# Eight attention pairs scored on row halves, weight splits on VectorE, and another slot order in the expert stage

## The chip, the cores and the metric

One NeuronCore of a Trainium2 chip runs the whole program. The metric is the device time of one execution in microseconds (us); lower is better. A profiled execution gives a trace beside its time. A change of 0.5%, about 4 us here, is what a measurement of this kernel can tell from none.

## The reference

Three stages, each fed by the one before it.

```
# attention: q, k, v are (4, 12, 448, 64)
scores = cap * tanh(q @ k.T / sqrt(64) / cap)
attn = exp(scores - max) / (sum + 1e-9);  x = attn @ v
# dense layer: x (1792, 768), w_in (768, 1024), w_out (1024, 768)
h = x @ w_in;  s = h * softmax(h);  ln = (s - mean) / sqrt(var + 1e-6) * g_ln
x = ln @ w_out
# experts: 8 of them, one per token
e = argmax(x @ w_gate + modality_bias[modality_id])
out = probs[e] * (relu(x @ w1[e]) @ w2[e])
```

w_in and w_out arrive as 64-bit floats.

## The kernel before, in words

**Attention** walks over 24 pairs of heads (batch b, pair p, n = 6b + p). `a_load` fetches K and Q of a pair, head dimension on the partitions; two heads of 64 fill 128. `a_sc` makes scores for one head j and two of four key chunks of 112 keys (cp selects the two), ScalarE (ACT) turns them by Tanh and Exp into a tile "e" (L688, L689), and `a_av` multiplies e by V (L710, tile "av") and sums the exponentials into the tile "S": directly with a 0/1 matrix ("zone") where `direct` holds (n < 6, L718), or, for later pairs, over sums that VectorE (DVE) and GpSimd (POOL) formed first (L695 to L699, L726).

Products on TensorE (PE) are either plain fp32 or split into a rounded fp32r part and a remainder. `a_split` makes these for K (tiles kh, kl) and Q (qs, high part above and low part below). Pairs 0 and 1 are "plain": fp32, K stored twice on the two partition halves, Q with zeros in the lower half. Pair 2 is in `HALF`: both heads in one tile, split, three products on 64 partitions each. Pairs 3 to 23 are split, two products of 128 partitions per chunk.

**Weights.** While the first pairs run, 12 pieces of w_in and 16 of w_out are loaded by POOL's queue and turned to fp32 by three DVE instructions (`f64_to_f32`, L433 to L435). `conv_in` then rounds (L459, ACT, two on DVE) and forms the remainder winl on POOL (L460). `conv_out` does it with g_ln folded in (L478 or L480, then L481), `conv_tr` transposes the piece on PE (L490, tile "pt") and copies it out (L492), `conv_og` forms eight gate columns (L498, tile "po"; L499, L500). `CUS` says behind which half pair each piece stands. The tables KHA, QSA, KLP, QLP, ESP, CIN, COUT, WTD name the engine of each piece of work.

**Dense layer.** Once a batch's six pairs are done (`a_fin1`, `a_fin2`), its token tiles are cut into small steps, which `fill` puts between the attention products of later pairs: h = x w_in (L540 to L542), activation, transposes, y = ln w_out (L590 to L592). Up to here a scheduler sets each engine's order from the program; from the expert stage on the program's order is kept.

**Experts.** A busiest expert's first tokens go first; then the slots of `STATIC` follow: D (4 x 128 tokens), F (2 x 128), H (128), each with its own expert's w1 and w2 loaded by the SP queue, rounded on ACT (L1025) and the remainder on DVE (L1026). `SMALL` hangs two slots T of 32 tokens on slots 0 and 2. A slot is: transposes of the gathered tokens (`s_tr`, tiles xtD, xtH, xtF, L1056), the first product (`s_h`, L1079 to L1081, tile phD or phF; for H `s_hh`, L1099 to L1101, followed by transposes `s_ht`, tile htH, L1115), the second product (`s_o`, L1146 to L1148, tiles poD, poH, poF). A T slot has `t_tr` (tile tpT, L1170), `t_h` (thT, L1181), `t_ht` (ttT, L1191, copied to hTT, L1193) and `t_o` (toT, L1204). `run_slots` sets their order; the transposes of the next slot stand between the two products of the present one.

Every engine takes its instructions in order; the ring of tiles "e" has 4 buffers, scores and most other PSUM tiles share 3.

Of the kernel before, what the change touches and what calls it, by code (L numbers as in the profile page):

```python
# [10 lines left out]
F32 = mybir.dt.float32  # L11
# [53 lines left out]
HALF = (2,)  # L65
BIN = 0
BOUT = -1
QLP = (1, 8, 10, 11, 13)
CIN = (1, 5)
# [3 lines left out]
FFIRST = 0  # L73
KHA = (6, 7, 8, 11)
QSA = (2, 8, 11, 15, 23)
KLP = (4, 5, 6, 8, 9, 10, 12, 13, 15, 16, 18, 19, 22, 23)
ESP = (3, 5, 6, 7, 9, 19, 20, 21, 22)
XHA = (0, 2, 3, 5, 7, 9, 11, 12)
XLP = (1, 3, 4, 6, 9, 10)
WTD = (1, 2, 6, 8, 12, 14, 15)  # L80
XCD = (6, 7, 9, 10, 12, 13, 14, 15, 16, 17, 18, 19, 20)
QACT = 0
VACT = 0
COUT = (0, 2, 3, 4, 5, 6, 8, 9, 10, 11, 12, 14)
CUS = (0, 3, 3, 3, 4, 4, 5, 5, 5, 5, 5, 6, 7, 7, 8, 8, 9, 9, 10, 11, 11, 12, 12, 13, 13, 14, 14, 15, 16, 17)
# [5 lines left out]
def attn_moe_kernel(ctx, tc, qt, kt, vv, cap, w_in, w_out, g_ln, ids, w_gate, mbias, w1, w2, out):  # L91
# [357 lines left out]
    def conv_in(k, hf):  # L449
        raw = mp.tile([P, 512, 2], I32, tag="m4", name=f"rawi{k}_{hf}", bufs=4)  # L450
        pool.dma_start(out=raw, in_=w_in[k * P:(k + 1) * P, hf * 512:(hf + 1) * 512]
                     .bitcast(I32).rearrange("p (f t) -> p f t", t=2))
        t = mp.tile([P, 512], I32, tag="x3", name=f"ti{k}_{hf}", bufs=4)
        f64_to_f32(t, raw)
        tf = t.bitcast(F32)
        h_, l_ = winh[k][:, hf * 512:(hf + 1) * 512], winl[k][:, hf * 512:(hf + 1) * 512]

        def rest():
            (dve.tensor_copy if (2 * k + hf) in CIN else act.copy)(h_, tf)  # L459
            pool.tensor_sub(l_, tf, h_)  # L460

        defer(BIN, rest)
# [3 lines left out]
    def conv_out(c, hf):  # L466
# [8 lines left out]

        def rest():
# [4 lines left out]
            dve.scalar_tensor_tensor(l_, tf, g_t[:, c:c + 1], h_, op0=ALU.mult, op1=ALU.subtract)  # L481

        defer(BOUT, rest)
        wT[c, hf] = tf

    def conv_tr(c, hf):
# [5 lines left out]
        (dve.tensor_copy if 2 * c + hf in WTD else act.copy)(tt, pt[:, :3 * P].rearrange("p (a b) -> p a b", a=3))  # L492
# [119 lines left out]
    def plain(b, p):  # L612
        return b * NP + p < PLAIN and b * NP + p not in HALF

    def a_load(b, p):
        k, q = [], []
        if b * NP + p in HALF:
            for l, src, nm in ((k, kt, "k"), (q, qt, "q")):
                t = ap_.tile([P, S], F32, tag="raw", name=f"{nm}r{b}_{p}", bufs=4)
                sp.dma_start(out=t, in_=src[b, p].rearrange("j d s -> (j d) s"))  # L620
                l += [t, t]
            raws[b, p] = (k, q)
            return
# [18 lines left out]
    def a_split(b, p, js=(0, 1)):  # L642
        k, q = raws[b, p]
        spl.setdefault((b, p), [])
        for j in js:
            n = b * NP + p
            if n in HALF:
                if j == js[0] and not spl[b, p]:
                    kh = ap_.tile([P, S], F32R, tag="kh", name=f"kh{b}_{p}", bufs=3)
                    kl = ap_.tile([P, S], F32R, tag="kl", name=f"kl{b}_{p}", bufs=3)  # L650
                    qh = ap_.tile([P, S], F32R, tag="qs", name=f"qh{b}_{p}", bufs=3)
                    ql = ap_.tile([P, S], F32R, tag="qs", name=f"ql{b}_{p}", bufs=3)
                    (act.copy if n in KHA else dve.tensor_copy)(kh, k[j])
                    (act.copy if n in QSA else dve.tensor_copy)(qh, q[j])
                    (pool if n in KLP else dve).tensor_sub(kl, k[j], kh)
                    (pool if n in QLP else dve).tensor_sub(ql, q[j], qh)
                    spl[b, p] = [(kh, kl, (qh, ql))] * 2
                continue
            if plain(b, p):
                spl[b, p].append((k[j], None, q[j]))  # L660
                continue
# [3 lines left out]
            n = b * NP + p  # L665
# [7 lines left out]

    def a_sc(b, p, j, cp):
        kh, kl, qs = spl[b, p][j]
        ps = atile(f"sc{b}_{p}_{j}_{cp}")
        for c in range(2):
            k0 = (2 * cp + c) * CK
            if b * NP + p in HALF:
                r = slice(64 * j, 64 * j + 64)  # L680
                for i, (x, y) in enumerate(((kh, qs[0]), (kl, qs[0]), (kh, qs[1]))):
                    pe.matmul(ps[:CK, c, :S], x[r, k0:k0 + CK], y[r], start=(i == 0), stop=(i == 2))
                continue
            pe.matmul(ps[:CK, c, :S], kh[:, k0:k0 + CK], qs, start=True, stop=plain(b, p))  # L684
            if not plain(b, p):
                pe.matmul(ps[:CK, c, :S], kl[:, k0:k0 + CK], qs, start=False, stop=True)  # L686
# [14 lines left out]
    avt, spt = {}, {}  # L701

    def a_av(b, p, cp):
        if cp == 0:
            avt[b, p] = btile(f"av{b}_{p}")
        o = avt[b, p]
        v = vt[b, p]
        for c in range(2):
            for j in range(2):
                pe.matmul(o[64 * j:64 * j + 64, :S], v[:, 2 * cp + c, 64 * j:64 * j + 64],  # L710
                          et[b, p, j, cp][:, c, :], start=(cp == 0 and c == 0), stop=(cp == 1 and c == 1))
        if cp == 0 and p == 0:
            spt[b] = psS.tile([P, 512], F32, tag="S", name=f"S{b}")
        if direct(b, p):
            for j in range(2):
                for c in range(2):
                    g = 2 * j + c
                    pe.matmul(spt[b][32 * g:32 * g + 32, :S], zone[:, 31 - p:63 - p], et[b, p, j, cp][:, c, :],  # L718
                              start=(p == 0 and cp == 0), stop=(p == NP - 1 and cp == 1))
        if cp == 1:  # L720
            (dve.tensor_copy if b * NP + p in XCD else act.copy)(xtile(b)[:, p, :], o[:, :S])
        if cp == 1 and p % 2 and not direct(b, p):
# [669 lines left out]
```

## Time and profile before

| | |
|---|---|
| median of 3 runs | 815.36 us (812.24 to 815.41) |
| profiled execution, its own time | 816.4 us |
| its span, first to last instruction | 814.6 us |
| PE busy | 770.6 us (95%) |
| DVE busy | 478.4 us (59%) |
| ACT busy | 389.8 us (48%) |
| POOL busy | 260.1 us (32%) |
| mean granted PE clock | 0.97 of full |

Shares of the whole span are averages over stages with different limits. The view by windows gives each engine's busy time in a stretch, and the granted clock of PE there; a mean clock between 0.5 and 1 is a mixture of its two levels, 1.2 and 2.4 GHz. The durations of matmuls in the trace overlap, since they are pipelined: what one costs in a row of them is the distance between starts.

### The profile page before, as it was taken

The numbers are of one execution on the slowest core, as the hardware profiler recorded it, in microseconds if no ns is written. First come the engines' busy times: TensorE is split into PE (matmuls) and PEld (weight loads), VectorE is DVE, ScalarE is ACT, GpSimd is POOL, SyncE is SP. The second block draws the span as 40 slices with busy tenths as digits, with TensorE's granted clock in tenths as the row PEclk, the third lists the DMA queues.
The fourth block names the chain that finished last, engine by engine and source line by source line (L and its number), as shares of the span: only waits on it lengthen the run. The fifth ranks groups of instructions, "written<-read, shape, count | busy, mean of one in ns | idle before, by whom it ended". The sixth has DMA issues, their size and how long they took to land.

```text
span 814.6 us, 11543 instructions
## 1 busy us (share of the span) xinstructions
PE 770.6 (95%) x4158; PEld 593.0 (73%) x4158; DVE 478.4 (59%) x843; ACT 389.8 (48%) x539; POOL 260.1 (32%) x325
## 2 busy tenths in 40 slices
PE   7888989999999999999999999899999989999983
PEld 2324545676677877577769799799879978799982
DVE  4999897757764566675435755756146171461730
ACT  5665853766755545656651224434144252442530
POOL 3763244544443342438623213441200101001000
PEclk9979979999999999999999999999999989999997
DMA  7866532123322222223000302467928259382711
GB/s 187 253 190 188 175 110 55 47 76 99 97 70 65 77 57 76 88 63 94 12 20 20 138 20 97 153 229 245 387 81 258 104 201 394 130 259 103 239 66 42
DMA packets 41206, 107.28 MB, mean 132 GB/s; under 512 B 7047, under 2 KB 18833, under 8 KB 41138
## 3 DMA queue, kind: packets, MB, share of 16 engines
q1 hardware_dynamic: 34610, 77.01, 29.8%
q0 software_dynamic: 6528, 29.42, 10.4%
q8 instruction: 35, 0.57, 0.3%
q14 instruction: 33, 0.27, 0.1%
HBM read 95.33 MB, written 11.27 MB: 131 GB/s over the span
## 4 chain that ended last, share of the span: by engine, by line
PE 79%; DVE 9%; DMA 5%; issue 3%; ACT 2%; SPq 1%; POOL 0%; POOLq 0%; DVEq 0%; ACTq 0%
PE av L710 8%; PE h L540 5%; PE y L590 5%; PE h L542 5%; PE y L591 5%; PE h L541 5%; PE y L592 5%; PE sc L684 4%; PE sc L686 4%; PE poD L1146 3%; PE poD L1148 3%; PE poD L1147 3%; PE phD L1080 3%; PE phD L1081 3%; PE phD L1079 3%
## 5 line engine op out<-in xcount | busy, mean ns | idle before, releaser
L688 ACT ACTIVATE e<-sc,sc 112x896 f32<-112x896 f32 x96 | 95.8, 1005 | 81.9 <-PE sc L686 67.5
L689 ACT ACTIVATE e<-e,cap_t 112x896 f32<-112x896 f32 x96 | 99.1, 1043 | 1.2
L710 PE MATMUL av<-e,v 112*64 112x448 f32 x384 | 97.4, 577 | 1.9 <-ACT e L689 1.0
L590 PE MATMUL y<-wouh,lh 128*128 128x388 f32 x224 | 77.6, 346 | 1.8 <-ACT lh L580 1.8
L592 PE MATMUL y<-wouh,ll 128*128 128x388 f32 x224 | 76.1, 340 | 0.3 <-DVE ll L581 0.2
L591 PE MATMUL y<-woul,lh 128*128 128x388 f32 x224 | 76.0, 339 | 0.0
L540 PE MATMUL h<-winh,xh 128*128 128x512 f32 x168 | 69.4, 413 | 0.2
L684 PE MATMUL sc<-qs,kh 128*112 128x448 f32 x168 | 64.7, 385 | 4.3 <-DVE qs L668 3.0
L542 PE MATMUL h<-winh,xl 128*128 128x512 f32 x168 | 66.7, 397 | 0.2 <-DVE xl L528 0.2
L541 PE MATMUL h<-winl,xh 128*128 128x512 f32 x168 | 66.3, 395 | 0.0
L686 PE MATMUL sc<-qs,kl 128*112 128x448 f32 x168 | 62.8, 374 | 0.0
L710 PEld LDWEIGHTS av<-e,v 112*64 112x64 f32 x384 | 26.3, 140 | 45.9 <-issue 36.5
L699 POOL TENSOR_TENSOR es<-es,et 112x448 f32<-112x448 f32 x36 | 45.4, 1263 | 28.0 <-DVE et L698 27.1
L669 POOL TENSOR_TENSOR kl<-kr,kh 128x448 fp32r<-128x448 f32 x28 | 34.5, 1232 | 52.8 <-PE sc L686 20.1
L590 PEld LDWEIGHTS y<-wouh,lh 128*128 128x128 f32 x224 | 42.1, 188 | 12.1 <-issue 7.9
L1026 DVE TENSOR_TENSOR wl_H<-raw_H,wh_H 128x768 fp32r<-128x768 f32 (+1 forms) x28 | 29.1, 1070 | 36.9 <-ACT wh_H L1025 36.9
L540 PEld LDWEIGHTS h<-winh,xh 128*128 128x128 f32 x168 | 31.6, 188 | 18.9 <-issue 10.7
L1026 DVE TENSOR_TENSOR wl_D<-raw_D,wh_D 128x768 fp32r<-128x768 f32 (+1 forms) x28 | 29.9, 1071 | 24.9 <-ACT wh_D L1025 23.5
L668 DVE TENSOR_TENSOR qs<-qr,qs 64x448 fp32r<-64x448 f32 x42 | 39.2, 934 | 6.5 <-ACT qs L667 5.3
L1146 PE MATMUL poD<-wh_D,hhD 128*128 128x384 f32 x128 | 43.0, 336 | 0.0
L1148 PE MATMUL poD<-wh_D,hlD 128*128 128x384 f32 x128 | 42.8, 334 | 0.0
L1147 PE MATMUL poD<-wl_D,hhD 128*128 128x384 f32 x128 | 42.8, 334 | 0.0
(392 smaller groups left out, 1811.5 us busy)
## 6 DMA issues: line engine op xcount, KB each, us to landing
kr<-in_kt_dram SPq DMA_DIRECT2D x92, 112.0 KB, 2.5
qr<-in_qt_dram SPq DMA_DIRECT2D x88, 112.0 KB, 2.9
rawi<-in_w_in_dram POOLq DMA_DIRECT2D x12, 512.0 KB, 4.8
rawo<-in_w_out_dram POOLq DMA_DIRECT2D x16, 384.0 KB, 4.0
raw_D<-in_w_dram SPq DMA_DIRECT2D x12, 512.0 KB, 3.6
wr_T<-in_w_dram SPq DMA_DIRECT2D x16, 384.0 KB, 4.1
raw_D<-in_w_dram SPq DMA_DIRECT2D x16, 384.0 KB, 4.8
wr_T<-in_w_dram SPq DMA_DIRECT2D x12, 512.0 KB
```

The lines of the kernel that those rows point to most:

```text
L540: pe.matmul(o, s["xh"][d], winh[d][:, c], start=(d == 0), stop=False)
L541: pe.matmul(o, s["xh"][d], winl[d][:, c], start=False, stop=False)
L542: pe.matmul(o, s["xl"][d], winh[d][:, c], start=False, stop=(d == ND - 1))
L590: pe.matmul(o, s["lh"][f], wouh[f][:, c], start=(f == 0), stop=False)
L591: pe.matmul(o, s["lh"][f], woul[f][:, c], start=False, stop=False)
L592: pe.matmul(o, s["ll"][f], wouh[f][:, c], start=False, stop=(f == NF - 1))
L684: pe.matmul(ps[:CK, c, :S], kh[:, k0:k0 + CK], qs, start=True, stop=plain(b, p))
L686: pe.matmul(ps[:CK, c, :S], kl[:, k0:k0 + CK], qs, start=False, stop=True)
L688: act.activation(e, ps[:CK, :, :S], AF.Tanh, scale=sc8[:CK])
L689: act.activation(e, e, AF.Exp, scale=cap_t[:CK])
L710: pe.matmul(o[64 * j:64 * j + 64, :S], v[:, 2 * cp + c, 64 * j:64 * j + 64], et[b, p, j, cp][:, c, :], start=(cp == 0 and c == 0), stop=(c ...
L1146: pe.matmul(p, hh[:, f, o], wh[:, c], start=(f == 0), stop=False)
```

## The change

Pairs 0 to 7 become plain (`PLAIN = 8`) and direct (`DIRECT = 8`). A plain pair loads K and Q once, as 128 partitions with both heads, and `a_scp` multiplies each head on its own 64 partitions, the two heads one behind the other, in fp32, with no split. The products with V and the sums of a pair are one block, `a_av`, which now stands behind the first score group of the next pair. The ring of "e" gets 5 buffers. In `conv_in` the rounding is on ACT throughout and the remainder on DVE; in `conv_out` both are on DVE; the copies of the transposed pieces are on ACT. `CUS` becomes regular, two pieces per half pair.

In the expert stage F comes ahead of the second H, `t_ht` stands between two halves of the next slot's first transposes with its copy on ACT, and `t_tr` of the second T slot is cut: the scaling of its tokens (`t_sc`) stays, the transposes move into `s_o`, ahead of the third slice from the end.

Core of the diff:

```diff
-STATIC = [("D", 0), ("H", 0), ("D", 1), ("H", 1), ("F", 0)]
+STATIC = [("D", 0), ("H", 0), ("D", 1), ("F", 0), ("H", 1)]
-PLAIN = 3
-DIRECT = 6
+PLAIN = 8
+DIRECT = 8
...
-HALF = (2,)
-CIN = (1, 5)
...
-CUS = (0, 3, 3, 3, 4, 4, 5, 5, 5, 5, 5, 6, 7, 7, 8, 8, 9, 9, 10, 11, 11, 12, 12, 13, 13, 14, 14, 15, 16, 17)
+CUS = (0, 0, 1, 1, 2, 2, 3, 3, 4, 4, 5, 5, 6, 6, 7, 7, 8, 8, 9, 9, 10, 10, 11, 11, 12, 12, 13, 13, 14, 14)
...
-            (dve.tensor_copy if (2 * k + hf) in CIN else act.copy)(h_, tf)
-            pool.tensor_sub(l_, tf, h_)
+            act.copy(h_, tf)
+            dve.tensor_sub(l_, tf, h_)
...
-            if 2 * c + hf in COUT:
-                dve.tensor_scalar(h_, tf, g_t[:, c:c + 1], None, op0=ALU.mult)
-            else:
-                act.activation(h_, tf, AF.Copy, scale=g_t[:, c:c + 1])
+        dve.tensor_scalar(h_, tf, g_t[:, c:c + 1], None, op0=ALU.mult)
...
-        (dve.tensor_copy if 2 * c + hf in WTD else act.copy)(tt, pt[:, :3 * P].rearrange("p (a b) -> p a b", a=3))
+        act.copy(tt, pt[:, :3 * P].rearrange("p (a b) -> p a b", a=3))
...
+    def a_scp(b, p, cp):
+        k, q = raws[b, p]
+        chunks = (2 * cp, 2 * cp + 1)
+        ps = [atile(f"sc{b}_{p}_{c}") for c in chunks]
+        for c, t in zip(chunks, ps):
+            for j in range(2):
+                r = slice(64 * j, 64 * j + 64)
+                pe.matmul(t[:CK, j, :S], k[r, c * CK:c * CK + CK], q[r], start=True, stop=True)
+        es = [e_new(f"e{b}_{p}_{c}") for c in chunks]
+        for e, t in zip(es, ps):
+            act.activation(e, t[:CK, :, :S], AF.Tanh, scale=sc8[:CK])
+        for c, e in zip(chunks, es):
+            act.activation(e, e, AF.Exp, scale=cap_t[:CK])
...
         else:
-            r = ap_.tile([CK, S], F32, tag="es", name=f"et{b}_{p}_{j}", bufs=6)
-            (pool if b * NP + p in ESP else dve).tensor_add(r, e[:, 0, :], e[:, 1, :])
-            pool.tensor_add(est[b, p, j], est[b, p, j], r)
+            dve.tensor_add(est[b, p, j], est[b, p, j], e[:, 0, :])
+            pool.tensor_add(est[b, p, j], est[b, p, j], e[:, 1, :])
...
         for cp in range(2):
-            for j in range(2):
-                a_sc(b, p, j, cp)
-                deferred(j)
-                fill(FW[j])
...
+            if plain(b, p):
+                a_scp(b, p, cp)
+            else:
+                a_sc(b, p, 0, cp)
+            if cp == 0 and n:
+                a_av(*pairs[n - 1])
...
-            if n or cp:
-                pb, pp, pc = (b, p, 0) if cp else (*pairs[n - 1], 1)
-                a_av(pb, pp, pc)
...
-        dve.tensor_copy(h, pt)
+        act.copy(h, pt)
...
+                if f == NF - 3 and late_:
+                    late_()
...
-            if t:
+            elif t:
+                s_tr(nx, (0,), (0,))
                 t_ht(t)
+                s_tr(nx, (0,), (1,))
+                s_tr(nx, (1, 2, 3))
+            elif nx:
+                s_tr(nx)
             if tn:
-                t_tr(tn)
+                t_sc(tn)
...
-            s_o(s, step, n == len(seq) - 1)
+            s_o(s, step, n == len(seq) - 1, (lambda: t_tr(tn)) if tn else None)
```

What moves in the order of the engines, at three places. In these rows a name such as sc_1_0 carries the pair within its batch first; the last number of a name counts tiles.

PE, from the first scores of pair 1, before (sc_pair_head_cp):

```order
L684 MATMUL sc_1_0_0_250<-qr_1_0_164,kr_1_0_161 112x448 x2
L684 MATMUL sc_1_1_0_264<-qr_1_1_170,kr_1_1_167 112x448 x2
L710 MATMUL av_0_240<-e_0_0_1_225,v_0_159 64x448
L710 MATMUL av_0_240<-e_0_1_1_233,v_0_159 64x448
L710 MATMUL av_0_240<-e_0_0_1_225,v_0_159 64x448
L710 MATMUL av_0_240<-e_0_1_1_233,v_0_159 64x448
L718 MATMUL S_245<-e_0_0_1_225,zone 32x448 x2
L718 MATMUL S_245<-e_0_1_1_233,zone 32x448 x2
L684 MATMUL sc_1_0_1_282<-qr_1_0_164,kr_1_0_161 112x448 x2
```

and now (sc_pair_chunk, one row for both heads):

```order
L653 MATMUL sc_1_0_244<-qr_1_155,kr_1_153 112x448 x2
L653 MATMUL sc_1_1_245<-qr_1_155,kr_1_153 112x448 x2
L689 MATMUL av_0_256<-e_0_0_192,v_0_151 64x448 x2
L689 MATMUL av_0_256<-e_0_1_193,v_0_151 64x448 x2
L689 MATMUL av_0_256<-e_0_2_218,v_0_151 64x448 x2
L689 MATMUL av_0_256<-e_0_3_219,v_0_151 64x448 x2
L697 MATMUL S_265<-e_0_0_192,zone 32x448 x2
L697 MATMUL S_265<-e_0_1_193,zone 32x448 x2
L697 MATMUL S_265<-e_0_2_218,zone 32x448 x2
L697 MATMUL S_265<-e_0_3_219,zone 32x448 x2
L653 MATMUL sc_1_2_294<-qr_1_155,kr_1_153 112x448 x2
```

The products with V and the sums of pair 0 are one block of 16 between the two score groups of pair 1, where two blocks of 8 stood.

POOL in the conversions, before:

```order
L460 TENSOR_TENSOR winl_127<-ti_0_379,winh_121 128x512
L451 DMA rawi_1_459<-in_w_in_dram 128x1024
L460 TENSOR_TENSOR winl_127<-ti_1_385,winh_121 128x512
L451 DMA rawi_0_465<-in_w_in_dram 128x1024
L460 TENSOR_TENSOR winl_128<-ti_0_443,winh_122 128x512
L451 DMA rawi_1_515<-in_w_in_dram 128x1024
L460 TENSOR_TENSOR winl_128<-ti_1_449,winh_122 128x512
```

and DVE at the same pieces now:

```order
L452 TENSOR_TENSOR winl_127<-ti_0_284,winh_121 128x512
L452 TENSOR_TENSOR winl_127<-ti_1_290,winh_121 128x512
L427 SCALAR_TENSOR_TENSOR ti_0_316<-rawi_0_314,ti_0_316 128x512
L425 TENSOR_SCALAR ti_1_322<-rawi_1_320 128x512
L425 TENSOR_SCALAR ti_0_364<-rawi_0_362 128x512
L426 SCALAR_TENSOR_TENSOR ti_1_322<-rawi_1_320,ti_1_322 128x512
L426 SCALAR_TENSOR_TENSOR ti_0_364<-rawi_0_362,ti_0_364 128x512
```

POOL has only the loads left at this place; the remainders stand in DVE's order, behind ACT's rounding.

PE in slot H0 of the expert stage, before:

```order
L1101 MATMUL phH_1_5936<-wh_H_5_5709,xl_H_5552 128x512
L1056 MATMUL xtD_0_0_5978<-ident,ygD_0_5573 128x128 x3
L1056 MATMUL xtD_0_1_5984<-ident,ygD_0_5573 128x128 x3
L1115 MATMUL htH_0_5993<-ident,huH_5937 128x128 x4
L1115 MATMUL htH_1_6000<-ident,huH_5937 128x128 x4
L1056 MATMUL xtD_1_0_6007<-ident,ygD_1_5577 128x128 x3
...
L1056 MATMUL xtD_3_1_6039<-ident,ygD_3_5585 128x128 x3
L1170 MATMUL tpT_6051<-ident,ygT_5228 128x32 x6
L1146 MATMUL poH_0_0_6064<-wh_H_0_5787,hhH_5991 128x384
```

and now the place of tpT:

```order
L1132 MATMUL poH_0_1_5830<-wh_H_4_5629,hlH_5762 128x384
L1157 MATMUL tpT_5915<-ident,ygT_4998 128x32 x6
L1130 MATMUL poH_0_0_5829<-wh_H_5_5842,hhH_5761 128x384
L1131 MATMUL poH_0_0_5829<-wl_H_5_5843,hhH_5761 128x384
L1132 MATMUL poH_0_0_5829<-wh_H_5_5842,hlH_5762 128x384
```

The transposes of the second T slot no longer stand ahead of the slot's second product but behind five of its eight slices.

## Rows read from the trace of the kernel before

**Rows 1.** Windows: length, then busy (count) of PE, PEld, DVE, ACT, POOL; clock, DMA, GB/s.

```profile
40.00:60.00 20.00, 17.01 (x60) 5.96 (x58) 18.29 (x26) 12.46 (x17) 11.62 (x12) 0.70 0.66 197
100.00:120.00 20.00, 17.03 (x74) 9.58 (x74) 19.71 (x33) 10.90 (x18) 8.41 (x9) 0.75 0.36 105
200.00:240.00 40.00, 40.00 (x201) 27.52 (x200) 28.98 (x49) 25.86 (x34) 18.45 (x19) 1.00 0.31 91
```

**Rows 2.** Timeline, start and us first: ACT's first Tanh; PE's first dense product.

```profile
8.50 1.01 ACT L688 ACTIVATE e<-sc,sc 112x896 f32<-112x896 f32 x1 [5.44 <-PE sc L684]
...
127.40 0.50 PE L540 MATMUL h<-winh,xh 128*128 128x512 f32 x1
```

**Rows 3.** Timeline of PE in half a plain pair: scores, products with V, sums.

```profile
16.70 3.26 PE L684 MATMUL sc<-qr,kr 128*112 128x448 f32 x8
19.89 1.72 PE L710 MATMUL av<-e,v 112*64 112x448 f32 x8
21.54 0.96 PE L718 MATMUL S<-e,zone 112*32 112x448 f32 x8
```

**Rows 4.** Timeline of PE in pair 2: across the change of head, and within one head.

```profile
28.97 0.47 PE L682 MATMUL sc<-qh,kl 64*112 64x448 f32 x2
29.17 0.47 PE L682 MATMUL sc<-ql,kh 64*112 64x448 f32 x2
...
34.01 0.37 PE L682 MATMUL sc<-ql,kh 64*112 64x448 f32 x1
34.22 0.36 PE L682 MATMUL sc<-qh,kh 64*112 64x448 f32 x1
```

**Rows 5.** By line: us min/median/max of one, first and last start; DVE, POOL, POOL's loads.

```profile
L433 DVE TENSOR_SCALAR ti<-rawi x12: 411/432/1929, 17.9 to 55.6; 128x512 int32<-128x512 int32 x12
L434 DVE SCALAR_TENSOR_TENSOR ti<-rawi,ti x12: 677/692/1948, 18.4 to 56.7; 128x512 int32<-128x512 int32 x12
L435 DVE SCALAR_TENSOR_TENSOR ti<-rawi,ti x12: 671/682/3147, 19.3 to 58.5; 128x512 int32<-128x512 int32 x12
L460 POOL TENSOR_TENSOR winl<-ti,winh x12: 1275/1315/3621, 21.0 to 63.3; 128x512 fp32r<-128x512 f32 x12
L481 DVE SCALAR_TENSOR_TENSOR woul<-to,g_t,wouh x16: 544/611/5208, 65.0 to 141.9; 128x384 fp32r<-128x384 f32 x16
L451 POOL DMA_DIRECT2D rawi<-in_w_in_dram x12: 527/700/764, 8.9 to 44.3; - x12
```

**Rows 6.** Groups by line, ACT: count, busy us, mean ns, idle before.

```profile
L689 ACT ACTIVATE e<-e,cap_t 112x896 f32<-112x896 f32 x96 | 99.1, 1043 | 1.2
L688 ACT ACTIVATE e<-sc,sc 112x896 f32<-112x896 f32 x96 | 95.8, 1005 | 81.9 <-PE sc L686 67.5 <-PE sc L684 7.5 <-POOL et L698 3.8
L459 ACT CAST winh<-ti 128x512 fp32r<-128x512 f32 x10 | 6.2, 618 | 13.8 <-DVE ti L435 13.8
L492 ACT COPY wT<-pt 128x384 f32<-128x384 f32 x9 | 4.3, 476 | 4.2 <-PE pt L490 2.0 <-PE po L498 1.9
```

**Rows 7.** Timeline of PE, one transposed piece of w_out and its gate columns.

```profile
80.04 0.55 PE L490 MATMUL pt<-ident,to 128*128 128x128 f32 x3
80.43 1.40 PE L498 MATMUL po<-wg_t,wT 128*128 128x8 f32 x12
```

**Rows 8.** Windows of 10 us in the expert stage, columns as in rows 1.

```profile
600.00:610.00 10.00, 8.32 (x129) 6.23 (x122) 3.34 (x8) 3.58 (x8) 2.01 (x2) 1.00 0.15 41
650.00:660.00 10.00, 6.04 (x41) 5.77 (x40) 7.27 (x20) 6.32 (x15) 1.04 (x1) 0.80 0.14 40
780.00:790.00 10.00, 8.27 (x37) 7.95 (x38) 4.07 (x6) 2.67 (x5) 0.00 (x0) 0.83 0.01 2
```

**Rows 9.** Timeline of PE in the expert stage: idle time before, and its releaser.

```profile
605.00 2.81 PE L1204 MATMUL toT<-wr_T,hTT 128*32 128x192 f32 x64 [1.68 <-DVE hTT L1193]
...
656.96 0.82 PE L1170 MATMUL tpT<-ident,ygT 32*128 32x32 f32 x6 [3.96 <-issue]
...
781.26 0.44 PE L1146 MATMUL poF<-wh_F,hhF 128*128 128x384 f32 x1 [1.73 <-ACT hhF L1084]
```

More of the change, by code (lines that the diff above doesn't have):

```diff
@@ L642, in a_split @@
     def a_split(b, p, js=(0, 1)):
+        if plain(b, p):
+            return
         k, q = raws[b, p]
         spl.setdefault((b, p), [])
+        n = b * NP + p
         for j in js:
[L646 to L661, printed above, removed]
             kh = ap_.tile([P, S], F32R, tag="kh", name=f"kh{b}_{p}_{j}", bufs=3)
@@ L678, in a_sc @@
             k0 = (2 * cp + c) * CK
[L679 to L686, printed above, removed]
@@ L713, in a_av @@
             spt[b] = psS.tile([P, 512], F32, tag="S", name=f"S{b}")
         if direct(b, p):
-            for j in range(2):
[L716 to L721, printed above, removed]
@@ L722, in a_av @@
-        if cp == 1 and p % 2 and not direct(b, p):
+            for c in range(4):
+                for j in range(2):
+                    g = 2 * j + c % 2
+                    pe.matmul(spt[b][32 * g:32 * g + 32, :S], zone[:, 31 - p:63 - p], et[b, p, j, c],
+                              start=(p == 0 and c < 2), stop=(p == NP - 1 and c > 1))
+        elif p % 2:
             for j in range(2):
@@ L829, in attn_moe_kernel @@
         for cp in range(2):
[L830 to L836 removed]
+            if plain(b, p):
+                a_scp(b, p, cp)
[3 more added lines that the diff above has]
+                a_av(*pairs[n - 1])
+            deferred(0)
+            fill(FW[0])
+            if cp == 0 and n + 1 < len(pairs):
+                a_split(*pairs[n + 1], js=(0,))
+            if not plain(b, p):
+                a_sc(b, p, 1, cp)
+            fill(FW[1])
+            if cp == 1 and n + 1 < len(pairs):
+                a_split(*pairs[n + 1], js=(1,))
             if cp == 1 and n + 2 < len(pairs):
                 a_load(*pairs[n + 2])
[L839 to L841 removed]
             if cp == 0 and n + 1 < len(pairs):
@@ L849, in attn_moe_kernel @@
                 convs.pop(0)[1]()
-            if b > 0 and not FFIRST:
+            if b > 0:
                 finish(b - 1, 2 * p + cp)
-    a_av(B - 1, NP - 1, 1)
+    a_av(B - 1, NP - 1)
     fill(2)
@@ L1038, in s_gather, with s_tr @@
         ss[s] = {"g": gs, "ga": ga}
-    def s_tr(s, part=range(4)):
+    def s_tr(s, part=range(4), halves=(0, 1)):
         nm = sname(s)
         n = len(cols(s))
-        if 0 in part:
+        if 0 in part and 0 in halves:
             ss[s]["xh"] = g2.tile([P, ND, n * P], F32R, tag="xh2", name=f"xh2_{nm}")
@@ L1051, in s_tr @@
             o = slice(i * P, (i + 1) * P)
-            for q in range(2):
+            for q in halves:
                 pt = ctile(f"xt{nm}_{i}_{q}").rearrange("p (b c) -> p b c", c=P)
@@ L1058, in s_tr @@
                 dve.tensor_sub(xl[:, r, o], pt[:, :3, :], xh[:, r, o])
-            dve.tensor_scalar(ga[:, i:i + 1], g[:, DM:DM + 1], 1e-9, None, op0=ALU.add)
-        if n - 1 in part:
+            if 1 in halves:
+                dve.tensor_scalar(ga[:, i:i + 1], g[:, DM:DM + 1], 1e-9, None, op0=ALU.add)
+        if n - 1 in part and 1 in halves:
             dve.reciprocal(ga[:, :n], ga[:, :n])
```

99 lines of the change are left out of this document (42 added, 57 removed).

## The prediction

> **What bounds the kernel now.** I read the windows first. From 200 to 240 us PE is busy for 40.00 of 40.00 us at clock 1.00 [rows 1]: there its own products set the time. From 40 to 60 us it is another picture: DVE is busy for 18.29 of 20 us, PE for 17.01 at a mean clock of 0.70; from 100 to 120 DVE 19.71, PE 17.03, clock 0.75. A mean of 0.70 is a mixture of the two levels, 12 of 20 us at 1.2 GHz, which cost 6 us of work; 0.75 is 10 us, or 5 lost. So early on PE waits for what DVE prepares, is then slow when it could work, and the dense products, which are what fills PE later, cannot start before their weights and the first batch's six pairs are through: the first one stands at 127.40 us [rows 2]. Whatever brings that date forward shortens the kernel, less the PE work that is only displaced. In the expert stage the windows around 600, 650 and 780 us show PE busy for 8.32, 6.04 and 8.27 of 10 us [rows 8], and the timeline names single gaps there: 1.68 us for the copy hTT, 3.96 us ahead of tpT, 1.73 us for hhF in the last slot [rows 9].
>
> **Early stage, what goes.** The splits of pairs 2 to 7 go, and POOL does no more remainders. The latter matters beyond POOL: the three DVE instructions of a w_in piece have medians of 0.432, 0.692 and 0.682 us but reach 1.93, 1.95 and 3.15 us, POOL's subtraction 1.315 at the median and 3.62 at most [rows 5]; the two stretch each other. I take medians for what remains on DVE.
>
> **Early stage, what DVE now has.** A w_in half piece: 0.432 + 0.692 + 0.682 plus the new remainder, 0.81 as an estimate (L481's 0.611 for 384 columns, times 512/384), 2.6 us; 12 of them 31 us. A w_out half piece: the same three on three quarters of the columns, 1.35, the scaling now on DVE, about 0.32 (three quarters of L433), and L481's 0.611: 2.3 us; 16 of them 37 us. Together 68; begun at 17.9 us [rows 5] they could be done by 86. DVE is no longer last.
>
> **Early stage, the chain that is last next.** ACT then: begun at 8.50 us [rows 2], and ahead of the first dense product come seven and a half pairs of four Tanh and four Exp on 896 columns, 30 x (1.005 + 1.043) = 61.4 us [rows 6]; 12 roundings at 0.618, 7.4; 16 copies of transposed pieces at 0.476, 7.6 [rows 6]; and some 20 smaller instructions (copies of the first batch's result, gate columns, pair 8's high parts), 8.5 as an estimate from those 0.476. That gives 93.4.
>
> PE has to follow. In a plain pair's half it now takes 3.26 us for eight score records, 1.65 from start to start for eight products with V, 0.96 for the sums [rows 3]. Score products on separate halves of the rows can run side by side: in pair 2, two products take 0.20 us at the change of head (28.97 to 29.17), one takes 0.21 within a head (34.01 to 34.22) [rows 4]. So the scores of a half pair fall from 3.26 to about 1.65, and a pair costs 3.3 + 3.3 + 1.9 = 8.5 us of PE, close to ACT's 8.2. While w_out pieces stand between the pairs, four transposes at 0.39 and two sets of gate products at 1.40 [rows 7] add 4.4: 12.9 us against ACT's 11.1, so PE is last there by 1.8 us over four pairs, 7 us. I add 5 us for the first pairs, where ACT would stand at the twelfth piece at about 45 us and DVE is done with it only at 17.9 + 31 = 49, and 3 us for one fall of the clock, half of what a 20 us window loses now. The first dense product comes at 93.4 + 7 + 5 + 3 = 108.4, **19 us earlier**. About 1 us of PE work that now stands behind that product moves ahead of it: 20 us gained.
>
> At one place a row and a rule could part. Each w_in load's issue takes POOL 0.700 us at the median, 0.764 at most [rows 5], though DVE is nearly full: nothing here stretches a load. The Trainium skill ("SBUF — State Buffer", section "SBUF: two separate sides") says that a transfer issued from POOL's queue can starve for its descriptors while DVE holds the port pair that both share, 620 ns alone becoming some 3100. By that rule DVE's new work would delay the loads; the rows show the stretching between POOL's and DVE's arithmetic only, and by them the sum stands.
>
> **The steady stage.** From pair 8 on PE has the same products; the additions that move between DVE and POOL cost nothing as long as both have the slack that 28.98 and 18.45 of 40 us leave [rows 1]. If that cover went, an addition of 1.3 us per chunk (as L460's) could show; I take 0. The block of products with V now stands behind the next pair's first scores; the fifth buffer of e holds what it reads meanwhile. The bounds are 0 and about 6 us lost, one window's loss [rows 1].
>
> **Expert stage.** t_ht between two halves of transposes hides hTT's wait: 1.68 and, for the second T slot, 1.0 as an estimate, 2.7 us; at least 1.5, as the cover is three transposes. tpT now follows five of eight slices, when its scaled tokens are long there: its 3.96 us go, and with them about 2 of the half-clocked 4 us in that window (clock 0.80 [rows 8]), 6.0; at least 3, at most 7. With H last, F's 1.73 and the slow stretch at 0.83 (3.4 us at 1.2 GHz, 1.7 lost) go, 3.4; but the last slot's chain from its first product over ReLU, the four transposes and their copy to the second product is now bare where the next slot's transposes covered it. That is 0 to 3.4, I take 1.2, so 2.2 gained, between 0 and 3.4. Together **11 us**, between 4 and 14.
>
> **Sum.** 816.4 (the profiled execution's own time) - 20 - 11 = 785.4. That execution stands 1 us above the median of 815.36; I say 785.
>
> **Rivals.**
>
> *Halves not side by side.* The change then doesn't do what it says: scores in fp32 cost 3.2 us per half pair, where the rows for pair 2 are of another kind of product and overlap only at one place per group. 3.1 us more for each of five pairs in which PE is last, 15.5: 801. Chance 0.13.
>
> *The clock stays low for part of the stage.* PE, ACT and DVE hand each other small blocks; in the windows where PE was busy for 17 of 20 us its clock was 0.70 [rows 1]. Two more such losses of 5 to 6 us: 796. Against it: PE's share grows. Chance 0.13.
>
> *Loads late on POOL's queue.* If each of the 12 loads were stretched by up to 2.5 us, as L435's longest (3.147 against 0.682 [rows 5]), pieces would come every 3.1 us rather than 2.6, 6 us later: 791. This is the place of the rule above; the rows speak against it. Chance 0.08.
>
> *Expert gains stay out*, since the gaps move to the instruction behind (hhF's place taken by the last slot's chain, tpT's by its copy): 2 of 11 are left, 794. Chance 0.06.
>
> *Slower.* The ring of e holds five tiles and a pair fills four, so the second Tanh group of a pair waits until the products and sums of the pair before have read theirs. With PE at 1.2 GHz a pair costs 17 us (0 to 2) or 25.8 (3 to 6), which no other engine can cover: 8.5 + 3 x 17 + 4 x 25.8 = 163 us, the first dense product at about 165 and, with the expert gain, 842. This decides once over some 62 us more of the early stage run at half clock, since 62 / 2 eats the 31 gained. For it: clocks of 0.70 and 0.75 now [rows 1]; against it: those come from waits for DVE, which go. Chance 0.08.
>
> *Little or nothing comes of both parts*, 806 to 820: 0.04.
>
> **How the numbers follow.** The forecast has 0.48, with its own range of 775 to 793 (early gain 16 to 26, expert gain 7 to 14). The range of 772 to 806 adds the four rivals on the faster side and leaves out the slower one, the last one and some edge. 0.5%, about 4 us, is what a measurement of this kernel can tell from no change: faster takes all of the forecast and the first four rivals but 0.02, 0.86; slower 0.08; the rest, 0.06, is the same.
>
> **What would show it.** Right: eight score records of a half pair in about 1.65 us; the first dense product near 108 us; DVE's conversions at their medians, and POOL with loads alone among them; a mean clock above 0.9 between 20 and 100 us; toT with less than 0.5 us of idle time, tpT with none; the last slot with about 1.2 us ahead of its second product. Wrong: scores that still take 3.2 us, load issues above 2 us on POOL, a clock near 0.7 for most of the first 100 us, or additions of DVE or POOL that PE waits for behind 200 us.

## The result and the profile after

| | before | after |
|---|---|---|
| median of the runs | 814.63 us | 792.63 us (790.94 to 794.49) |
| ratio, with its 95% interval | | 0.9729 (0.9699 to 0.976) |
| span of the profiled execution | 814.6 us | 791.4 us |
| PE busy | 770.6 us | 750.9 us |
| DVE, POOL busy | 478.4, 260.1 us | 445.3, 208.8 us |

The time fell by 22 us. The forecast was 785 within 772 to 806: the range holds it, the forecast itself was 7.6 us too low. The last product of the dense layer (y, low part) divides the span into the two stages that the change touches, the early stage (attention with the conversions of weights, and the dense layer) and the expert stage. The timeline of PE, before and then after:

```profile
524.12 0.34 PE L592 MATMUL y<-wouh,ll 128*128 128x388 f32 x1
```

```profile
509.49 0.34 PE L577 MATMUL y<-wouh,ll 128*128 128x388 f32 x1
```

So 14.6 us were won by then. The two spans differ by 23.2 us (814.6 - 791.4), so the other 23.2 - 14.6 = 8.6 us were won behind it. One more window of the kernel before, with the columns of [rows 1]:

```profile
20.00:40.00 20.00, 17.74 (x83) 7.26 (x85) 19.52 (x27) 14.14 (x18) 14.96 (x12) 0.95 0.83 251
```

and the windows of the changed kernel:

```profile
20.00:40.00 20.00, 15.24 (x64) 4.59 (x64) 17.36 (x33) 16.53 (x22) 4.66 (x8) 0.74 0.81 269
40.00:60.00 20.00, 15.96 (x76) 6.26 (x77) 18.06 (x39) 15.42 (x22) 5.26 (x8) 0.91 0.64 196
60.00:80.00 20.00, 20.00 (x124) 9.90 (x121) 13.99 (x30) 15.09 (x23) 4.46 (x7) 1.00 0.53 152
100.00:120.00 20.00, 19.11 (x95) 9.94 (x95) 10.82 (x21) 12.18 (x18) 1.24 (x1) 1.00 0.12 35
200.00:240.00 40.00, 40.00 (x190) 27.36 (x189) 27.11 (x49) 23.79 (x31) 15.28 (x17) 1.00 0.23 68
```

DVE is as busy as before from 40 to 60 us (18.06 of 20 us, 18.29 in [rows 1]) and much less from 100 to 120 us (10.82, it was 19.71). From 60 us on PE is nearly full at full clock. From 20 to 40 us it is less busy than before, at a mean clock of 0.74 in place of 0.95. The steady window is as full as before. The rows that answer to [rows 2, 3] are the first Tanh, the scores, products with V and sums of an early pair, and the first dense product, from the timelines of ACT and PE:

```profile
6.50 1.01 ACT L656 ACTIVATE e<-sc,sc 112x896 f32<-112x896 f32 x1 [3.43 <-PE sc L653]
...
57.50 1.76 PE L653 MATMUL sc<-qr,kr 64*112 64x448 f32 x8
59.19 1.72 PE L689 MATMUL av<-e,v 112*64 112x448 f32 x6
60.84 1.71 PE L697 MATMUL S<-e,zone 112*32 112x448 f32 x16
...
116.29 0.50 PE L525 MATMUL h<-winh,xh 128*128 128x512 f32 x1
```

Eight score records take 1.69 us from start to start where they took 3.2 [rows 3], and the sums of a whole pair 1.64 where each of two blocks took 0.96. The first dense product comes 11.1 us earlier than the 127.40 of [rows 2]. How that gain is made up is seen in windows that end at the first dense product, before and after:

```profile
0.00:127.40 127.40, 111.22 (x482) 50.97 (x482) 109.69 (x190) 80.32 (x109) 59.05 (x68) 0.91 0.61 178
```

```profile
0.00:116.30 116.30, 99.61 (x517) 42.20 (x517) 79.08 (x172) 80.76 (x112) 23.45 (x42) 0.94 0.57 175
```

PE idles as long as before: 127.40 - 111.22 = 16.2 us, now 16.7. What shrank is its busy time, by 11.6 us. By the mean clock, at most 0.09 x 127.4 = 11.5 us of work were lost to half clock (1.2 GHz) and now at most 0.06 x 116.3 = 7.0. By this estimate some 4.5 us are clock and the other 7 are work that is gone; the scores of pairs 0 and 1 alone are four half pairs x 1.5 = 6.0. This is bookkeeping of one execution each: it doesn't say what PE would have waited for without the relief of DVE, which an experiment below does.

In the expert stage, with [rows 9] beside it, toT starts with no idle time and tpT with none (where a row names no idle time, there is none to speak of); a new wait stands in D1's first product:

```profile
589.39 2.81 PE L1191 MATMUL toT<-wr_T,hTT 128*32 128x192 f32 x64
...
642.55 0.55 PE L1157 MATMUL tpT<-ident,ygT 32*128 32x32 f32 x6
...
652.37 0.57 PE L1061 MATMUL phD<-xh_D,wh_D 128*128 128x512 f32 x1 [2.48 <-ACT txT L1158]
```

### The profile page after: what moved, and what is told of

Read it like the earlier page. It is cut to its first block, busy times and chain, and to the rows that moved or that the text cites. A ratio compares the mean times of both kernels' runs of the same rounds, so it can differ in the third digit from the quotient of the medians.

```text
span 791.4 us, 11415 instructions
## 1 busy us (share of the span) xinstructions
PE 750.9 (95%) x4174; PEld 578.3 (73%) x4174; DVE 445.3 (56%) x821; ACT 391.3 (49%) x541; POOL 208.8 (26%) x285
## 4 chain that ended last, share of the span: by engine, by line
PE 81%; DVE 6%; issue 4%; DMA 3%; ACT 2%; POOL 1%; SPq 0%; POOLq 0%; DVEq 0%; ACTq 0%
PE av L689 9%; PE h L525 5%; PE h L527 5%; PE h L526 5%; PE y L575 5%; PE y L576 5%; PE y L577 4%; PE sc L667 3%; PE sc L668 3%; PE poD L1130 3%; PE poD L1132 3%; PE poD L1131 3%; PE phD L1061 3%; PE phD L1062 3%; PE phD L1063 3%
## 5 line engine op out<-in xcount | busy, mean ns | idle before, releaser
L670 ACT ACTIVATE e<-sc,sc 112x896 f32<-112x896 f32 x64 | 64.5, 1007 | 84.7 <-PE sc L668 82.5
L689 PE MATMUL av<-e,v 112*64 112x448 f32 x384 | 95.4, 560 | 3.2 <-ACT e L658 2.2
L671 ACT ACTIVATE e<-e,cap_t 112x896 f32<-112x896 f32 x64 | 66.9, 1045 | 1.2
L689 PEld LDWEIGHTS av<-e,v 112*64 112x64 f32 x384 | 27.3, 138 | 49.3 <-issue 40.0
L679 POOL TENSOR_TENSOR es<-es,e 112x448 f32<-112x448 f32 x32 | 41.6, 1299 | 34.5 <-DVE es L678 34.4
L667 PE MATMUL sc<-qs,kh 128*112 128x448 f32 x128 | 47.7, 372 | 0.0
L668 PE MATMUL sc<-qs,kl 128*112 128x448 f32 x128 | 46.8, 366 | 0.0
L653 PE MATMUL sc<-qr,kr 64*112 64x448 f32 x128 | 32.7, 633 | 11.5 <-ACT e L656 6.9
L637 POOL TENSOR_TENSOR kl<-kr,kh 128x448 fp32r<-128x448 f32 x22 | 26.9, 1224 | 59.9 <-DVE kh L634 34.5
L576 PEld LDWEIGHTS y<-woul,lh 128*128 128x128 f32 x224 | 42.1, 188 | 0.8
```

What stands on the lines that cost most here:

```text
L576: pe.matmul(o, s["lh"][f], woul[f][:, c], start=False, stop=False)
L689: pe.matmul(o[64 * j:64 * j + 64, :S], v[:, c, 64 * j:64 * j + 64], et[b, p, j, c], start=(c == 0), stop=(c == 3))
```

## The experiments

Each kernel was timed beside the kernel before; how it stands to the changed kernel is taken from the two ratios, times 814.6 us. Where the 95% intervals of the two ratios overlap, the difference is at best at the edge of what can be told.

The two stages apart first. `early_alone` takes the expert stage of before, `expert_alone` the early stage of before.

```diff
-STATIC = [("D", 0), ("H", 0), ("D", 1), ("F", 0), ("H", 1)]
+STATIC = [("D", 0), ("H", 0), ("D", 1), ("H", 1), ("F", 0)]
...
-            s_o(s, step, n == len(seq) - 1, (lambda: t_tr(tn)) if tn else None)
+            s_o(s, step, n == len(seq) - 1)
```

(Two places of the edit of `early_alone`; it also takes back `t_ht`, its copy and `t_tr`.)

> The changed kernel with the expert stage of the kernel before (slot order, both edits of the T slots). By the two traces the last dense product stands 14.6 us earlier (523.8 against 509.1), so 814.6 - 14.6 = 800 us. The prediction's sum had 20 us for this part: 795. If the two parts lean on each other, it is neither, and early_alone and expert_alone do not add up to the whole 22 us.

> The kernel before with the changed expert stage alone. By the traces the stage behind the last dense product is 8.6 us shorter (23.2 of the span less 14.6): 814.6 - 8.6 = 806 us. The prediction's sum had 11 us: 803.6. The new wait of 2.48 us of the first product of D1, on the copy txT, should stand in this trace too.

Measured: 800.65 us, ratio 0.9818 (0.9791 to 0.9844), for `early_alone`, and 806.06 us, 0.9901 (0.9877 to 0.9925), for `expert_alone`. The product of the two ratios is 0.9721 against 0.9729 for both: the stages add up, and the sizes are those read from the trace, not the forecast's. In `expert_alone` D1's product waits 1.56 us on txT.

**The remainder on POOL again.**

```diff
-            dve.tensor_sub(l_, tf, h_)
+            pool.tensor_sub(l_, tf, h_)
```

> The changed kernel with the remainder of w_in on POOL again. Theory of the prediction: POOL's subtraction and DVE's three instructions stretch each other (means before 0.82, 0.95 and 1.00 against 0.42, 0.69 and 0.69 now), so DVE loses about 12 x 0.97 = 11.6 us and is spared 12 x 0.69 = 8.3: a few us later in the first 50 us, 793 to 797. Rival: the stretching came from other work, and DVE is spared 8.3 us in the stretch where ACT waits 7 us for it: 786 to 789.

799.42 us, 0.9804 (0.9779 to 0.9829): 6.1 us above the changed kernel, the direction of the first theory and more than it said. By line (us min/median/max of one, as in [rows 5]), the changed kernel and then this one:

```profile
L425 DVE TENSOR_SCALAR ti<-rawi x12: 420/422/428, 18.4 to 44.7; 128x512 int32<-128x512 int32 x12
L427 DVE SCALAR_TENSOR_TENSOR ti<-rawi,ti x12: 682/686/709, 19.6 to 46.5; 128x512 int32<-128x512 int32 x12
```

```profile
L427 DVE SCALAR_TENSOR_TENSOR ti<-rawi,ti x12: 691/1634/1645, 20.0 to 52.2; 128x512 int32<-128x512 int32 x12
L452 POOL TENSOR_TENSOR winl<-ti,winh x12: 1259/1445/1645, 21.4 to 54.7; 128x512 fp32r<-128x512 f32 x12
```

With the subtraction on POOL the second combination takes 1.634 us at the median, not 0.686: about as long as the longest of POOL's own instructions (1.645; median 1.445). The Trainium skill ("SBUF — State Buffer", section "Who interferes with whom") says that a DVE instruction with two inputs in SBUF contends with one of GpSimd that reads SBUF; these rows agree. POOL's loads now also stand behind its subtractions, but DVE's waits for loads grew only from 2.4 to 3.7 us behind the first load, while its last second combination starts 5.7 us later (52.2 for 46.5).

PE feels it as waits and as half clock, in the window up to this kernel's first dense product (124.3 us):

```profile
0.00:124.30 124.30, 102.47 (x517) 43.53 (x517) 84.89 (x160) 81.02 (x112) 38.90 (x54) 0.90 0.54 163
```

It idles for 21.8 us instead of 16.7, and at most 0.10 x 124.3 = 12.4 us of work are lost to half clock, not 7.0. So without this relief of DVE the shorter PE work would in part have been waited away. The other moves between the engines (w_out's conversion, the copies, `CUS`) and the eight fp32 pairs by themselves were not run apart.

**What PE's time is worth: every score product twice.**

```diff
-                pe.matmul(t[:CK, j, :S], k[r, c * CK:c * CK + CK], q[r], start=True, stop=True)
+                for _ in range(2):
+                    pe.matmul(t[:CK, j, :S], k[r, c * CK:c * CK + CK], q[r], start=True, stop=True)
```

> The changed kernel with every score product of the eight early pairs computed twice (the second overwrites the first), which gives a half pair's scores the 3.3 us that full rows took in the kernel before. PE gets 16 x 1.65 = 26 us more. In the last four pairs, where PE has no gap, all of it should land: 8 x 1.65 = 13 us; in the first 57 us PE idles for 15.6 us and hides some or all of the rest: 806 to 819. The prediction's rival on rows that do not overlap had 15.5 us more. If ACT and not PE sets the pace of these pairs, less than 6 us lands: below 799.

807.39 us, 0.9909 (0.988 to 0.9939), 14.7 us above the changed kernel. That is as much as the whole early gain, and close to the 15.5 that the prediction's rival on rows that do not overlap had, though in part by chance: the rival counted five pairs in full. It is more than a way back, too, since the split scores of pairs 3 to 7 had cost no more in the kernel before than the single ones here (four records in 0.82 us, 127.97 to 128.79, half of a half pair). Of 26 us more of PE work a little over half lands. The windows of the changed kernel up to the first dense product, split at 57.4 us:

```profile
0.00:57.40 57.40, 41.79 (x191) 14.53 (x191) 40.29 (x89) 41.33 (x52) 16.56 (x32) 0.88 0.78 244
57.40:116.30 58.90, 57.82 (x328) 27.66 (x327) 38.80 (x83) 39.43 (x60) 6.89 (x10) 1.00 0.36 107
```

15.6 us of PE's idle time lie in the first, and 1.1 in the second. With doubled scores the second runs to 132.7 us with PE busy for 75.25 of 75.30. PE sets the pace of the last four pairs.

**The order of the heads.** Scores in the order chunk 0 and 1 of head 0, then of head 1.

```diff
-        for c, t in zip(chunks, ps):
-            for j in range(2):
+        for j in range(2):
+            for c, t in zip(chunks, ps):
```

> The changed kernel with the score products of a half pair in another order: both chunks of head 0, then both of head 1. If products overlap only when neighbours stand on different halves of the rows, one of three changes between neighbours is left to overlap: 3 x 0.82 = 2.5 us per half pair in place of 1.65. PE is busy without gap from 57 to 116 us, eight half pairs: 0.8 x 8 = 6.5 us later, up to 13 if the first four pairs feel it too: 799 to 806. If the order of the heads is of no matter, 792.6.

804.65 us, 0.9882 (0.9831 to 0.9932): the loss lies in the expected range, but not for the expected reason. It is known only roughly, 8 to 17 us by the interval. PE and ACT of this kernel:

```profile
67.14 1.77 PE L653 MATMUL sc<-qr,kr 64*112 64x448 f32 x8
68.95 1.91 ACT L656 ACTIVATE e<-sc,sc 112x896 f32<-112x896 f32 x2 [1.43 <-PE sc L653]
```

The eight records still take 1.70 us to the next instruction. The first Tanh is later: 1.81 us behind the scores' start, where the changed kernel has 1.05 (57.50 to 58.55), as the signal that chunk 0 is done now comes at the end of all eight records. A theory made after the run, sixteen half pairs x 0.76 = 12.2 us, would fit the 12.5 lost by the ratios, but the windows speak against it. Up to the first dense product of this kernel, 5.7 us later than in the changed one:

```profile
0.00:122.00 122.00, 106.60 (x517) 43.61 (x517) 76.69 (x172) 79.35 (x112) 22.84 (x42) 0.96 0.55 166
```

PE idles for 15.4 us, no more than the 16.7 of the changed kernel; it is busy for 7.0 us more. Among PE's groups by line in these stretches, the sums differ most, first the changed kernel and then this one:

```profile
L697 PE MATMUL S<-e,zone 112*32 112x448 f32 x112 | 14.0, 546 | 0.0
```

```profile
L697 PE MATMUL S<-e,zone 112*32 112x448 f32 x112 | 19.9, 548 | 0.0
```

The same 112 records take 5.9 us more, because the scheduler cut a pair's sums into three pieces, here 0.87, 0.89 and 1.65 us to the next start, where a whole pair takes 1.64 us:

```profile
73.80 0.94 PE L697 MATMUL S<-e,zone 112*32 112x448 f32 x2
...
78.03 0.95 PE L697 MATMUL S<-e,zone 112*32 112x448 f32 x6
...
80.29 1.72 PE L697 MATMUL S<-e,zone 112*32 112x448 f32 x8
```

That is the size of the loss in the early stage of this execution, whose last y product starts at 515.30 us in place of 509.49. Why the median lost more isn't shown.

**Products with V kept whole.** In the changed kernel the conversions' transposes (pt) and gate products (po) cut into the products with V. The timeline of PE there:

```profile
52.80 0.97 PE L689 MATMUL av<-e,v 112*64 112x448 f32 x4
53.70 0.55 PE L475 MATMUL pt<-ident,to 128*128 128x128 f32 x3
54.17 0.96 PE L689 MATMUL av<-e,v 112*64 112x448 f32 x2
55.07 0.84 PE L483 MATMUL po<-wg_t,wT 128*128 128x8 f32 x6
```

Two products (four records) take 0.90 us to the next start, and one alone (two records) takes 0.90 as well. `av_whole` ties PE's order (`behind` makes a block follow the one before it in the program; scores and sums are tied as well), `turn_whole` adds the order of the heads above.

```diff
+        with behind(direct(b, p)):
             for c in range(4):
                 for j in range(2):
-                    pe.matmul(o[64 * j:64 * j + 64, :S], ...
+                    m = pe.matmul(o[64 * j:64 * j + 64, :S], ...
```

> The changed kernel with the order of PE tied, for the eight early pairs, so that the products with V and the sums of a pair stay one block; in the changed kernel the transposes and gate products of the conversions cut into them, and a product whose partner is cut off still takes 0.82 us. From 57.4 to 116.3 us the V products took 17.3 us where whole pairs would take 11.8 for the same 57 records (1.65 per eight), and the sums 8.4 where 6.6 would do: 7.3 us. Theory that cut pairs cost that: first dense product near 110, 786 to 789 us. Rival: the cuts fill time in which PE would wait for ACT's exponentials, so that the tied order waits instead: 791 to 796.

> av_whole with the heads in turn (both chunks of head 0, then both of head 1). heads_in_turn was 12 us slower than the changed kernel while eight score records took 1.70 us in either order. If that loss came from the sums and V products that the scheduler cut apart otherwise, the tied order takes it away: as av_whole within 2 us. If the order of the heads costs by itself, 6 us or more above av_whole.

800.78 us, 0.9818 (0.9785 to 0.9851), 7.3 us slower than the changed kernel, for `av_whole`, and 807.96 us, 0.992 (0.9894 to 0.9945), for `turn_whole`. The first theory of `av_whole` fell; its rival held, but for its size (791 to 796 us). The windows of `av_whole`:

```profile
80.00:100.00 20.00, 17.56 (x111) 9.87 (x108) 12.78 (x28) 13.38 (x22) 2.85 (x4) 0.91 0.43 118
100.00:120.00 20.00, 19.49 (x69) 11.11 (x67) 8.66 (x21) 8.33 (x12) 0.00 (x0) 0.57 0.09 24
...
0.00:124.70 124.70, 103.58 (x515) 48.15 (x515) 77.41 (x171) 81.62 (x112) 22.80 (x42) 0.84 0.54 163
```

PE idles for 21.1 us instead of 16.7, and after the gaps of 80 to 100 us the clock is 0.57: up to 0.16 x 124.7 = 20 us of work lost to half clock against 7.0. The products with V did become shorter by line (27.3 us busy in place of 33.9). So the pieces between them make them longer and yet keep PE fed. `turn_whole` lies 8.3 us above `av_whole`, so the order of the heads costs in the tied order too, where no sums are cut. Up to its first dense product (130.8 us) PE idles for 22.8 us and is busy for 108.0, against 21.1 and 103.6; whether the late first Tanh is the reason isn't shown.

**Four buffers of e.**

```diff
-        return ap_.tile([CK, 2, S], F32, tag="e", name=nm, bufs=5)
+        return ap_.tile([CK, 2, S], F32, tag="e", name=nm, bufs=4)
```

> The changed kernel with four buffers of e in place of five. The next pair's first Tanh then finds no free buffer until the products with V and the first sums of the pair before are through, some 4.2 us per pair behind its scores (3.3 for the V products, 0.9 for the first sums). Where ACT and PE hand on to each other pair by pair this lands almost whole: up to 8 x 4.2 = 33 us, 805 to 826. If the slack of ACT in the last four pairs (20 us of idle time) takes it up, 793 to 797.

798.01 us, 0.9775 (0.9747 to 0.9803): 3.7 us above the changed kernel by the ratios, 5.4 by the medians, nearest to the second case. The two intervals overlap a little, so the fifth buffer's worth is at the edge of what can be told; it is a small part of the 33 us of waiting that it was thought to hide.

**The new wait in the expert stage.** `copy_early` moves tpT three slices ahead and the scaling of its tokens to the slot's start; `copies_early` also keeps the roundings of the next slot back.

```diff
-                if f == NF - 3 and late_:
+                if f == NF - 6 and late_:
...
-QH = (6, 4)
+QH = (6, 6)
```

(The second part is in `copies_early` alone.)

> The changed kernel with the transposes tpT of the second T slot three slices earlier (and the scaling of its tokens ahead of the slot), so that their copy txT stands in ACT's order behind the first rounding of D1's weights and not behind the fifth. If the 2.48 us of the first product of D1 hang on that copy alone, they go, and with them 1.7 us of half clock: 788.5. Rival: the first product of D1 needs the banks of H0's result next, whose scaling obH on ACT stands behind the same roundings; then the wait only moves there: 791 to 793.

> As copy_early, and with fewer roundings pulled ahead in the second half of an H slot (6 in place of 4 slices left without them), so that obH too stands behind only one rounding of D1's weights on ACT. If both copies are what PE waits for, 788 to 789, and no idle time ahead of D1's products; if the weights of D1 themselves come too late, the wait is found at a rounding wh_D and the time stays at 791 to 793 or grows.

790.57 us, 0.9695 (0.9666 to 0.9723), for `copy_early`, and 789.38 us, 0.9674 (0.9644 to 0.9705), for `copies_early`. ACT of the changed kernel shows the cause, and PE of `copy_early` where the wait went:

```profile
649.13 1.05 ACT L1006 CAST wh_D<-raw_D 128x1024 fp32r<-128x1024 f32 x1 [0.76 <-DMA raw_D<-in_w_dram]
651.05 1.04 ACT L1006 CAST wh_D<-raw_D 128x1024 fp32r<-128x1024 f32 x1 [0.87 <-DMA raw_D<-in_w_dram]
652.01 0.31 ACT L1158 COPY txT<-tpT 128x192 f32<-128x192 f32 x1
```

```profile
650.26 0.50 PE L1061 MATMUL phD<-xh_D,wh_D 128*128 128x512 f32 x1 [0.81 <-ACT obH L1112]
651.57 0.50 PE L1061 MATMUL phD<-xh_D,wh_D 128*128 128x512 f32 x1 [0.33 <-DVE obH L1113]
```

tpT was done at 643, but its copy stood in ACT's order behind roundings that wait for loads, and the sixth output tile of D1 needs the bank of PSUM (the memory that products are written to) that the copy frees. With that copy moved, the next bank holds PE up for 0.81 and 0.33 us, as the rival said in part; with both ahead of the roundings no idle time is left there. The gains of 2.8 and 4.5 us over the changed kernel are at the edge of what the intervals tell; the gaps themselves are plain in the rows.

**Two tries at the early stage**, on top of `copies_early`: `late_copies` has each conversion half a pair later (CUS from 1 to 15), and `gates_on_dve` then has the gate columns' high part on DVE too.

```diff
-        act.activation(wouh[c][:, DM:YW], po[:, :NE], AF.Copy, scale=g_t[:, c:c + 1])
+        dve.tensor_scalar(wouh[c][:, DM:YW], po[:, :NE], g_t[:, c:c + 1], None, op0=ALU.mult)
```

> copies_early with each conversion one half pair later. In the changed kernel the first rounding of w_in stands in ACT's order ahead of pair 1's second Tanh and waits until 20.4 us for DVE, which waits for the load: 4.2 us in which ACT does nothing. If that wait is on the path, 2 to 4 us below copies_early: 785 to 787. Rival: what is put off comes back as later conversions ahead of the first dense product: 789 or more.

> late_copies with the high part of the eight gate columns formed on DVE in place of ACT. In the changed kernel ACT stands idle for 13.4 us up to the first dense product in front of these eight small instructions, waiting for the gate products on PE, with the next Tanh behind them in its order. If PE's own work sets the pace of the last four early pairs, as scores_twice says, ACT's wait costs nothing: 787 to 790, first dense product at 117 to 119. Rival: ACT's wait holds up the exponentials, and so PE's products are cut apart: 781 to 786.

788.52 us, 0.9662 (0.9639 to 0.9686), for `late_copies`, and 789.58 us, 0.9691 (0.9668 to 0.9714), for `gates_on_dve`. The first lies 1 us below `copies_early`, inside its interval. It says nothing on what ACT's early wait is worth, because the edit did not take the wait away. ACT's first rounding in the changed kernel and in `late_copies`:

```profile
20.36 0.62 ACT L451 CAST winh<-ti 128x512 fp32r<-128x512 f32 x1 [4.19 <-DVE ti L427]
```

```profile
20.78 0.62 ACT L451 CAST winh<-ti 128x512 fp32r<-128x512 f32 x1 [4.61 <-DVE ti L427]
```

`gates_on_dve` gains nothing over `late_copies`, as PE's pace says. Of all kernels run, `late_copies` is the fastest, and its interval lies below that of the changed kernel (from 0.9699).

## Why the prediction was right, and where it was short

**The direction and both parts held.** The scores of a half pair were said to fall to 1.65 us: 1.69. DVE's conversions of w_in run at their medians and POOL forms no remainders of w_in; put back there, they cost 6.1 us. The wait on POOL's queue did not come: a load's issue takes 0.540 us at the median (0.765 at most) where [rows 5] had 0.700, though the page of the profile has 5.7 us from issue to landing in place of 4.8. The Trainium skill ("SBUF — State Buffer", section "SBUF: two separate sides") says that descriptors starve while DVE runs an instruction in a mode that takes two ports; no issue of a w_in load was stretched here (of w_out's one took 1.053 us), and no run shows which mode DVE's instructions ran in. The slower rival, a ring of e that binds at half clock, needed 62 us more at half clock; the mean of 0.94 up to the first dense product (0.91 before) excludes it.

**The step that failed is the waits of ACT.** The working had 84.9 us of ACT's work behind a first Tanh at 8.50 us and 15 us of waits (5 for the first conversions, 7 where PE is last, 3 for the clock). Measured: first Tanh at 6.50 us, and ACT busy for 80.76 us up to 116.30, of which 1.5 precede the Tanh, so 79.3 of work. The waits are the rest, 116.3 - 6.5 - 79.3 = 30.5 us, twice what was put down. By the two windows split at 57.4 us, some 11 lie in the first four pairs, 4.19 of them in one place, ahead of ACT's first rounding (20.36 us), which waits for DVE, which waits for a load; what that wait is worth stays open, as `late_copies` kept it. The other 19.5 lie in the last four pairs, where 7 were put down, and 3 for the clock: PE needed 58.9 / 4 = 14.7 us for a pair, not 12.9. The sum had counted products with V and sums at the rate of whole blocks [rows 3]; in the order the scheduler made, they are cut by the pieces of the conversions. That cut products are slower is in the rows; that the time can be had back by keeping them whole was tried and is not so.

**The idea behind the early gain was only half right.** The prediction had PE waiting for DVE, and the gain as waits that go. PE idles for as long as before, 16 us; what is shorter is its work, less of it at half clock. Both halves were needed: with the scores twice the early gain is gone (14.7 us), and with DVE's relief taken back for w_in alone PE idles for 5.1 us more (6.1 us of time). The 14.6 us at the end of the dense layer, against 11.1 at its first product, are more than the 1 us of displaced work that the sum allowed: before, conversions ran on behind the first dense product (to 141.9 in [rows 5]), now they end ahead of it (the last remainder of w_out starts at 106.5).

**Expert stage: 8.6 in place of 11.** hTT's waits are gone as said. Of the 6.0 put down for tpT, 3.96 us of idle time went and 2.48 came back at D1 with a clock of 0.83 in that window, as tpT's copy was not followed into ACT's queue: the sum named where the transposes now stand, and not who frees their bank. For the last slot 1.2 us of bare chain were put down; the timeline has

```profile
766.75 0.39 PE L1083 MATMUL phH<-wh_H,xl_H 128*128 128x512 f32 x1
767.15 1.34 PE L1097 MATMUL htH<-ident,huH 128*128 128x128 f32 x8
768.48 0.45 PE L1130 MATMUL poH<-wh_H,hhH 128*128 128x384 f32 x1
```

with 1.5 us between the end of the one product (766.98, a product's 0.23 behind its start) and the start of the other. The eight transposes in it take 0.88 us in the slot before, where the next slot's transposes stand round them (634.40 to 635.28), so the wait itself is 0.6 us. With 0.27 us more ahead of the second product's third record (768.76 to 769.21, where 0.18 is usual) it comes to 0.9. The term was of the right size.

## What to carry to other kernels

Where a scheduler sets the order, a small change of the program can cut other blocks apart. Before a slower run is put down to a wait that is seen in it, compare the idle and busy time of the engine that sets the pace, and the busy time of each kind of its work: here a Tanh that came 0.76 us later was in plain sight, and PE's idle time had not grown; the same 112 sums took 19.9 us in place of 14.0. For the same reason, see in the trace that an edit took away the wait it was made for. Where an instruction is moved, follow the copy that frees its bank through the queue of the engine that does it, above all where that queue waits for loads. And small work that cuts PE's blocks apart may still be worth having, if without it PE pauses and its clock falls (0.94 to 0.84 here).

## What was not expected of the hardware

Four score products of 64 rows took 1.70 us in the order 0, 0, 1, 1 of the heads as in 0, 1, 0, 1: neighbours on the same half of the rows did not cost what one behind the other would (three steps of 0.82 were expected, 2.5). The single records of the trace start two by two in either order: at 67.139 and 67.153, then 67.606 and 67.619 us in the turned order, at 57.496 and 57.503, then 57.963 and 57.970 in the other. So products of the two halves seem to have run side by side although the program has two of one half first; that PE did not keep to the program's order between the halves is read from these starts alone. The signal to ACT yet came only at the end of the group. And one POOL subtraction per piece, spread over 33 us, more than doubled the median of DVE's second combination, by 0.95 us; that remainder on POOL cost the kernel 6.1 us.
